# RWKV attention with a routed expert layer on one core: r times the decay prefix on VectorE, half of the diagonals on ScalarE, r times k on GpSimd tied to a VectorE instruction, and the routing spread over two iterations

## The chip, the cores and the metric

The kernel runs on one NeuronCore of a Trainium2 chip. Five engines work side by side, each through a queue of its own in program order: TensorE (PE in the profile, its weight loads PEld), VectorE (DVE), ScalarE (ACT), GpSimd (POOL) and SyncE (SP), which here only issues DMAs. GpSimd issues the indirect DMAs. An instruction waits at the head of its engine's queue until the semaphores it names have been raised, and all behind it waits too. The metric is the device time of one execution in microseconds; the kernel before takes 459.83 us (median of three runs, 458.9 to 461.02).

## What is computed

A linear attention with a decaying state (batch 4, 8 heads, 768 steps, head dimension 48), and on its output a layer of 8 experts of which each token uses one:

```python
for t in range(S):
    cur = np.einsum('bhd,bhe->bhde', u[None] * kt, vt)
    y[:, :, t] = np.einsum('bhd,bhde->bhe', rt, state + cur)
    state = wt[:, :, :, None] * state + np.einsum('bhd,bhe->bhde', kt, vt)
...
logits = x @ w_gate
expert_idx = np.argmax(logits, axis=1)
...
for e in range(E):
    mask = expert_idx == e
...
    xe = x[mask]
    h = np.maximum(xe @ w1[e], 0.0)
    ye = h @ w2[e]
    out[mask] = gate_w[mask, None] * ye
```

## The kernel before

**Stages.** The first 191 us are the attention and the routing, the rest the experts: their weights are split into a high and a low part, tokens are gathered by expert, and the matrix products run back to back on TensorE. The change lies in the first part.

**Blocks.** The 768 steps are cut into 6 chunks of 128, and a chunk of one batch is a block: block n is chunk n // 4 of batch n % 4, 24 in all. A block holds all 8 heads: r, k and w lie as 112 partitions (two heads of a pair at partitions 0 and 64) by 4 pairs by 128 steps. VectorE makes a suffix product of the decays by a scan (`suf`, L331), its reciprocal (L335), `kh` = k times the suffix (L341) and a prefix product from that reciprocal (`pre`, L347). `rh` = r times the prefix (L315) is made by GpSimd but for block 0. TensorE multiplies kh with rh into two PSUM tiles `ap` (L454), one for each head of the pairs. The diagonal of the causal part is another number, r times k times u: GpSimd makes `rk` = r times k (L309), TensorE sums it over the dimension (`cp`, L431), ScalarE copies it (`cs`), TensorE turns it (`cpt`, L437), ScalarE copies it (`ct`), and GpSimd spreads it on the diagonal of `at` by two `affine_select` (L323), one for each half of the heads, with zeros elsewhere. VectorE then copies `ap` into `at` above the diagonal only, by two masked copies (L355). TensorE adds v times `at` (`av`, L488) to `yp`, in which the state's share (`pe_inter`, L466, with `g` from ScalarE) stands already. The state goes on through `kt`, `dp` (L479) and `sst` (L362): `sst` reads `dp` out of PSUM, and kp and dp share two PSUM buffers. ScalarE copies yp to `ytb`, TensorE turns it (`yq`, L495), ScalarE copies that into `xr`, the token rows.

**Order.** `iteration(n)` writes the order out by hand for TensorE, VectorE, ScalarE and GpSimd (`manual_schedule`), n from -3 to 23. One iteration works on several blocks: ap, the masked copies, the state and av of block n, the diagonals of block n + 1, suf, kh and pre of block n + 2, rk of block n + 3. What comes after the loop is placed by the scheduler, which also sets single instructions of it between those of the last iterations.

**Routing.** When a chunk's four blocks are done, its tokens are routed in the next chunk's iterations: at n % 4 == 0 the logits (L502) and `routing` on VectorE (maximum, exponentials on ScalarE, one-hot `oh`, the running counts `oa`, `ohacc`), at n % 4 == 1 `rank` on TensorE (L543 to L546), ahead of pe_inter, and `place` on VectorE, then one indirect scatter of GpSimd (L614) for each batch. From iteration 8 to 20 each iteration also splits a third of a piece of the first expert's weights, the high part by ScalarE, the low part by VectorE (L213).

**Dummy matmuls.** `keep_warm` (L111) issues matmuls of zeros into the unused part of a PSUM tile ahead of cp and of dp: six each in the first blocks, one each later.

## Time and profile before

| What | Value |
|---|---|
| Median of three runs | 459.83 us |
| The profiled execution | 459.9 us |
| Its span, first to last instruction | 458.1 us |
| Busy: PE, DVE, ACT, POOL | 419.8, 296.1, 199.8, 195.9 us |
| Mean granted TensorE clock | 0.934 |
| DMA queues, mean | 137 GB/s |
| First causal matmul of block 0, of block 23 | 15.2 us, 191.4 us |

The chain that ended last, followed back from the end, lies on PE for 68% of the span, on DVE for 13% and on DMA for 10%. In a timeline row stand the start in us, the length in us, the engine, the line, the operation, the tiles (written <- read), the shapes and how often; in brackets how long the engine was idle ahead of it and what ended that. Rows of several equal instructions are merged, and an instruction's length includes its start-up, which overlaps the one before by some 0.1 us; so a step's cost is read from start to start. A GpSimd or VectorE row is also as long as it is if the instruction was held after its start.

### The profile page before, as it was taken

What the parts mean: (1) busy time and instruction counts of PE and PEld (TensorE: products, weight loads), DVE (VectorE), ACT (ScalarE), POOL (GpSimd) and SP (SyncE); (2) the same over time, 40 slices, a digit from 0 to 9 for tenths busy, and PEclk for the clock granted to TensorE, in tenths of its full rate; (3) what the DMA queues carried; (4) which work ended last, traced back from release to release, by engine and by line L of the source; (5) the groups of instructions that cost most, each with busy time, mean ns of one, the idle gap of its engine ahead of it and who ended that gap; (6) DMA issues with size and microseconds to landing.
All of it is one profiled execution on the core that took longest, in us unless ns stands there. A gap on an engine that the chain in (4) does not pass through costs nothing.

```text
span 458.1 us, 9458 instructions
## 1 busy us (share of the span) xinstructions
PE 419.8 (92%) x3608; PEld 368.7 (80%) x3608; DVE 296.1 (65%) x514; ACT 199.8 (44%) x527; POOL 195.9 (43%) x176
## 2 busy tenths in 40 slices
PE   8888899889997996997799999999999999999991
PEld 5566687667765775796699998899999999999991
DVE  5979979999999998444666346345266363632320
ACT  3456455645564473443455344354254352522200
POOL 2998579579579585605401003004002052020530
PEclk9999779889799598799699999999999999999997
DMA  7999757658496314204936334624634455010021
GB/s 209 246 246 232 206 148 195 163 136 204 104 245 146 89 54 153 100 1 140 318 108 200 104 129 130 195 97 115 203 98 149 139 140 156 15 50 0 15 52 37
DMA packets 33178, 62.60 MB, mean 137 GB/s; under 512 B 8086, under 2 KB 21199, under 8 KB 33126
## 3 DMA queue, kind: packets, MB, share of 16 engines
q1 hardware_dynamic: 25222, 52.41, 41.8%
q0 software_dynamic: 7904, 9.52, 6.8%
q8 instruction: 30, 0.49, 0.5%
q14 instruction: 22, 0.18, 0.1%
HBM read 50.03 MB, written 12.29 MB: 136 GB/s over the span
## 4 chain that ended last, share of the span: by engine, by line
PE 68%; DVE 13%; DMA 10%; issue 4%; POOL 2%; SPq 1%; ACT 0%; DVEq 0%; POOLq 0%; ACTq 0%
PE bank L275 25%; PE bank L842 18%; PE opt L287 5%; DMA rkwt<-in_rkw_dram 4%; PE yp L466 4%; PE yp L488 3%; DMA vt<-in_vv_dram 3%; PE ap L454 3%; DVE pre L347 2%; DVE suf L331 2%; PE pt L266 2%; PE yq L495 2%; DVE kh L341 2%; PE op L831 2%; DVE at L355 1%
## 5 line engine op out<-in xcount | busy, mean ns | idle before, releaser
L237 POOL DMA_INDIRECT out_dram<-ot,xg x24 | 36.1, 1504 | 156.3 <-DVE ot L832 150.8
L275 PE MATMUL bank<-xl,w1h 128*128 128x448 f32 (+6 forms) x168 | 59.1, 356 | 0.0
L275 PE MATMUL bank<-xh,w1l 128*128 128x448 f32 (+6 forms) x168 | 58.1, 352 | 0.0
L275 PE MATMUL bank<-xh,w1h 128*128 128x448 f32 (+6 forms) x168 | 56.3, 358 | 0.0
L213 DVE TENSOR_TENSOR w2l<-wst,w2h 128x512 fp32r<-128x512 f32 x48 | 31.3, 685 | 36.5 <-ACT w2h L211 36.3
L278 DVE SCALAR_TENSOR_TENSOR hl<-bank,hh 128x192 fp32r<-128x192 f32 (+8 forms) x58 | 30.7, 539 | 33.1 <-ACT hh L277 33.0
L331 DVE TENSOR_TENSOR_SCAN suf<-rkwt,sufone 112x520 f32<-112x520 f32 x24 | 49.2, 2049 | 3.9 <-DMA rkwt<-in_rkw_dram 3.9
L614 POOL DMA_INDIRECT xs<-xr,pi x24 | 31.5, 1311 | 38.1 <-DVE pi L567 19.7
L277 ACT ACTIVATE hh<-bank 128x192 fp32r<-128x192 f32 (+8 forms) x58 | 26.9, 477 | 41.1 <-PE bank L275 40.8
L315 POOL TENSOR_TENSOR rh<-rkwt,pre 112x512 f32<-112x512 f32 x23 | 36.6, 1591 | 17.8 <-DVE pre L347 17.7
L323 POOL TENSOR_SCALAR_AFFINE_SELECT at<-ct 128x512 f32<-128x512 f32 x48 | 41.2, 881 | 0.0
L842 PE MATMUL bank<-hl,w2h 128*128 128x412 f32 (+5 forms) x114 | 40.8, 359 | 0.0
L842 PE MATMUL bank<-hh,w2l 128*128 128x412 f32 (+5 forms) x114 | 40.6, 358 | 0.0
L842 PE MATMUL bank<-hh,w2h 128*128 128x412 f32 (+5 forms) x114 | 39.8, 355 | 0.0
L309 POOL TENSOR_TENSOR rk<-rkwt 112x512 f32<-112x512 f32 x24 | 35.9, 1498 | 7.7 <-DMA rkwt<-in_rkw_dram 7.7
L355 DVE COPY_PREDICATED at<-cmask,ap 128x512 f32<-128x512 int32 x48 | 32.1, 722 | 7.4 <-PE ap L454 5.1
L488 PE MATMUL yp<-at,vt 128*48 128x128 f32 x384 | 32.6, 308 | 4.7 <-DVE at L355 4.7
L211 ACT ACTIVATE w1h<-wst 128x512 fp32r<-128x512 f32 x48 | 28.5, 627 | 16.4 <-PE bank L275 9.0
L847 ACT ACTIVATE oT<-bank 128x448 f32<-128x448 f32 (+5 forms) x18 | 9.4, 525 | 59.2 <-PE bank L842 59.2
L213 DVE TENSOR_TENSOR w1l<-wst,w1h 128x512 fp32r<-128x512 f32 x48 | 31.1, 686 | 6.4 <-ACT w1h L211 6.3
L347 DVE TENSOR_TENSOR_SCAN pre<-rkwt,pre 112x520 f32<-112x520 f32 x24 | 34.2, 1424 | 0.0
L275 PEld LDWEIGHTS bank<-xl,w1h 128*128 128x128 f32 x168 | 31.6, 188 | 1.1
(157 smaller groups left out, 939.0 us busy)
## 6 DMA issues: line engine op xcount, KB each, us to landing
wst<-in_w_dram SPq DMA_DIRECT2D x48, 256.0 KB, 4.8
...
```

Of the source, the lines that this page charges most:

```text
L213: nc.vector.tensor_tensor(out=lo, in0=st[:, cs], in1=hi.bitcast(F32), op=ALU.subtract)
L237: i = nc.gpsimd.indirect_dma_start(out=out[:, :], out_offset=bass.IndirectOffsetOnAxis(ap=t.bitcast(I32)[:, q, DM + 1:DM + 2], axis=0), in ...
L275: nc.tensor.matmul(hp, a, x[:, j, :], start=(i == 0), stop=(i == 8))
L309: nc.gpsimd.tensor_tensor(out=d["rk"], in0=d["r"], in1=d["k"], op=ALU.mult)
L315: (nc.vector if n == 0 else nc.gpsimd).tensor_tensor(out=d["rh"], in0=d["r"], in1=d["pre"][:, :, 0:C], op=ALU.mult)
L323: nc.gpsimd.affine_select(out=at[:, j], in_=co[:, j:H:2].unsqueeze(2).broadcast_to([P, NP_, C]), pattern=[[0, NP_], [-1, C]], compare_op=A ...
L331: nc.vector.tensor_tensor_scan(out=suf[:, ::-1], data0=d["w"][:, ::-1], data1=sufone.rearrange("p q c -> p (q c)")[:, ::-1], initial=0.0, ...
L347: nc.vector.tensor_tensor_scan(out=pre, data0=d["w"], data1=pre0[n % 2].rearrange("p q c -> p (q c)"), initial=0.0, op0=ALU.mult, op1=ALU.add)
L355: nc.vector.copy_predicated(out=d["at"][:, j], mask=cmask.unsqueeze(1).broadcast_to([P, NP_, C]), data=d["ap"][j])
L488: nc.tensor.matmul(d["yp"][64 * j:64 * j + D, q, :], d["v"][:, h * D:(h + 1) * D], d["at"][:, j, q, :], start=(n < B and q == 0), stop=(q ...
L614: i = nc.gpsimd.indirect_dma_start(out=xsf, out_offset=bass.IndirectOffsetOnAxis(ap=pi[:, b:b + 1], axis=0), in_=xr[:, b, :], in_offset=No ...
L842: nc.tensor.matmul(pp, w, a, start=(i == 0), stop=(i == 23))
```

## The change

- `rh` is made by VectorE for all blocks, at the end of the iteration that makes its prefix (block n + 2), where GpSimd made it an iteration later.
- Of the two diagonals of a block GpSimd makes one. The other is made by ScalarE: four activations, each the identity matrix (128x128) times a number per partition.
- `rk` stands near the head of GpSimd's iteration and, from iteration 0 on, waits for the reciprocal of block n + 2, behind which VectorE's masked copies stand. The diagonal stands behind it.
- `sst` of block n - 1 stands behind the masked copies of block n; it was at the end of iteration n - 1.
- `routing` is cut: the counts and the sums of the exponentials go into a new `count`, in the iteration after, behind the masked copies. `rank` moves behind cp (and its dummies) and ahead of kp. `place` loses what `count` took and moves behind `rh` and the weight split.
- The scatters of a chunk start an iteration later (n % 4 == 2), and two stand in the iteration with n % 4 == 0; the last chunk but one leaves two for after the loop.
- Ahead of cp and dp stand three dummies instead of one in the iterations with n % 4 == 0 and 1.

```diff
@@ pool_rk
-            nc.gpsimd.tensor_tensor(out=d["rk"], in0=d["r"], in1=d["k"], op=ALU.mult)
+            i = nc.gpsimd.tensor_tensor(out=d["rk"], in0=d["r"], in1=d["k"], op=ALU.mult)
+            if real(n - 3):
+                tc.add_manual_dep(i.ins, blk[n - 1]["rc"].name, mybir.DependencyInfo(
+                    mybir.DependencyClass.Sync, mybir.DependencyReason.DATA), reason="beside the copies of the causal part")
@@ pool_rh, now dve_rh
-            (nc.vector if n == 0 else nc.gpsimd).tensor_tensor(out=d["rh"], in0=d["r"], in1=d["pre"][:, :, 0:C], op=ALU.mult)
+            nc.vector.tensor_tensor(out=d["rh"], in0=d["r"], in1=d["pre"][:, :, 0:C], op=ALU.mult)
@@ pool_diag
-            for j in range(2):
-                nc.gpsimd.affine_select(out=at[:, j], in_=co[:, j:H:2].unsqueeze(2).broadcast_to([P, NP_, C]),
-                                        pattern=[[0, NP_], [-1, C]], compare_op=ALU.is_equal, fill=0.0, base=0, channel_multiplier=1)
+            nc.gpsimd.affine_select(out=blk[n]["at"][:, 0], in_=blk[n]["ct"][:, 0:H:2].unsqueeze(2).broadcast_to([P, NP_, C]),
+                                    pattern=[[0, NP_], [-1, C]], compare_op=ALU.is_equal, fill=0.0, base=0, channel_multiplier=1)
+    def act_diag(n):
+        if real(n):
+            for q in range(NP_):
+                nc.scalar.activation(blk[n]["at"][:, 1, q], ident, AF.Copy, scale=blk[n]["ct"][:, 2 * q + 1:2 * q + 2])
@@ pe_coef, pe_state
-            keep_warm(t[:, C:], 6 if n < B else 1)
+            keep_warm(t[:, C:], 6 if n < B else 3 if n % B in (2, 3) else 1)
-            keep_warm(t[:, NP_ * D:], 6 if n < B else 1)
+            keep_warm(t[:, NP_ * D:], 6 if n < B else 3 if n % B < 2 else 1)
@@ iteration
-        pool_rh(n + 1)
         dve_suf(n + 2)
         act_g(n + 1)
-        if route >= 0 and b == 1:
-            rank(route)
+        pool_rk(n + 3)
...
         pe_inter(n)
         dve_at(n)
+        dve_state(n - 1)
+        pool_diag(n + 1)
+        act_diag(n + 1)
...
+        if route >= 0 and b == 1:
+            count(route)
         pe_y(n - 1)
         dve_kh(n + 2)
         act_xr(n - 1)
         pe_coef(n + 2)
...
-        pool_diag(n + 1)
+        if route >= 0 and b == 1:
+            rank(route)
         pe_kt(n + 1)
...
-        pool_rk(n + 3)
-        dve_state(n)
+        dve_rh(n + 2)
```

How this moves the instructions on three engines follows in rows of the built programs: line, operation, tiles, shape of the output, and how often.

VectorE, in the iteration of block 13 (n % 4 == 1), from the masked copies on. Before:

```order
L355 COPY_PREDICATED at<-cmask,ap 128x512 x2
L341 TENSOR_TENSOR kh<-rkwt,suf 112x512
L557 TENSOR_REDUCE se<-ex 128x4
L558 TENSOR_SCALAR se<-se 128x4
L559 RECIPROCAL xr<-se 128x4
L560 COPY xr<-tokid 128x4
L562 TENSOR_TENSOR ps<-rank,ebase 128x32
L563 TENSOR_TENSOR ps<-ps,oh 128x32
L565 TENSOR_REDUCE pf<-ps 128x4
L567 CAST pi<-pf 128x4
L347 SCALAR_TENSOR_TENSOR pre<-rkwt,pre_1_177 112x520
```

After:

```order
L361 COPY_PREDICATED at<-cmask,ap 128x512 x2
L368 TENSOR_TENSOR sst_186<-dp,gbd_185 112x192
L541 CAST oa<-ohacc 128x8
L543 TENSOR_REDUCE ohs<-oh 128x8
L544 TENSOR_TENSOR ohacc<-ohacc,ohs 128x8
L546 TENSOR_REDUCE se<-ex 128x4
L547 TENSOR_SCALAR se<-se 128x4
L548 RECIPROCAL xr<-se 128x4
L549 COPY xr<-tokid 128x4
L347 TENSOR_TENSOR kh<-rkwt,suf 112x512
L353 SCALAR_TENSOR_TENSOR pre<-rkwt,pre_1_177 112x520
L319 TENSOR_TENSOR rh<-rkwt,pre 112x512
```

The state's update and the counts have come behind the copies, rh behind the prefix; the four instructions that read rank have gone from here to behind rh and the weight split.

GpSimd, with what each instruction waits for in brackets (DVE_49, PE_49 and the like are engines, DMAHW queues of loads). Before, from the first scatter of chunk 1 at the end of iteration 9 through iteration 10:

```order
L614 DMA xs<-xr,pi 24576x386 [waits DVE_49]
L315 TENSOR_TENSOR rh<-rkwt,pre 112x512 [waits DVE_49,Pool_49]
L323 AFFINE_SELECT at<-ct 128x512 [waits PE_49,Activation_49]
L323 AFFINE_SELECT at<-ct 128x512
L309 TENSOR_TENSOR rk<-rkwt 112x512 [waits DMAHW7_49,DMAHW0_49]
```

After, iteration 12 with its two scatters, and the head of the next:

```order
L309 TENSOR_TENSOR rk<-rkwt 112x512 [waits DMAHW5_49,DMAHW6_49,DVE_49,Pool_49]
L624 DMA xs<-xr,pi 24576x386
L325 AFFINE_SELECT at<-ct 128x512 [waits PE_49,Activation_49]
L624 DMA xs<-xr,pi 24576x386
L309 TENSOR_TENSOR rk<-rkwt 112x512 [waits DMAHW3_49,DMAHW4_49,DVE_49,Pool_49]
```

rh and one diagonal are gone, and rk, which waited for its block's load alone, has moved from behind the diagonals to the head and waits for VectorE (the reciprocal) as well.

TensorE, at the rank matmuls of the iteration of block 13. Before:

```order
L488 MATMUL yp<-at,vt 48x128 x8
L454 MATMUL ap<-rh,kh 128x128 x8
L543 LDWEIGHTS tri
L543 MATMUL rank<-oh,tri 128x32
L544 LDWEIGHTS ones
L544 MATMUL rank<-oa,ones 128x32
```

After, from the third dummy ahead of cp on (inter, yq and two dummies stand before these rows):

```order
L111 LDWEIGHTS ones
L111 MATMUL cp<-wz,ones 128x384
L437 MATMUL cp<-rk,ubt 32x128 x4
L559 LDWEIGHTS tri
L559 MATMUL rank<-oh,tri 128x32
L560 LDWEIGHTS ones
L560 MATMUL rank<-oa,ones 128x32
```

Rank stood directly behind ap, ahead of the block's other matmuls; now inter, yq, three dummies and cp stand ahead of it.

More of the change, by code (lines that the diff above doesn't have):

```diff
@@ L308, in pool_rk, with dve_rh @@
             d["rk"] = wk.tile([RP, NP_, C], F32, name="rk", tag="rk", bufs=4)
-            nc.gpsimd.tensor_tensor(out=d["rk"], in0=d["r"], in1=d["k"], op=ALU.mult)
-    def pool_rh(n):
+            i = nc.gpsimd.tensor_tensor(out=d["rk"], in0=d["r"], in1=d["k"], op=ALU.mult)
+            if real(n - 3):
+                tc.add_manual_dep(i.ins, blk[n - 1]["rc"].name, mybir.DependencyInfo(
+                    mybir.DependencyClass.Sync, mybir.DependencyReason.DATA), reason="beside the copies of the causal part")
+    def dve_rh(n):
         if real(n):
@@ L314, in pool_rh @@
             d["rh"] = wk.tile([RP, NP_, C], F32, name="rh", tag="rh", bufs=3)
[L315 removed]
+            nc.vector.tensor_tensor(out=d["rh"], in0=d["r"], in1=d["pre"][:, :, 0:C], op=ALU.mult)
     def pool_diag(n):
         if real(n):
[L320 to L325 removed]
+            blk[n]["at"] = wk.tile([P, 2, NP_, C], F32, name="at", tag="at")
+            nc.gpsimd.affine_select(out=blk[n]["at"][:, 0], in_=blk[n]["ct"][:, 0:H:2].unsqueeze(2).broadcast_to([P, NP_, C]),
[4 more added lines that the diff above has]
+                nc.scalar.activation(blk[n]["at"][:, 1, q], ident, AF.Copy, scale=blk[n]["ct"][:, 2 * q + 1:2 * q + 2])
     def dve_suf(n):
@@ L334, in dve_suf @@
             d["suf"] = suf.rearrange("p (q c) -> p q c", c=WP)
-            nc.vector.reciprocal(pre0[n % 2][:, :, 0:1], d["suf"][:, :, 1:2])
+            d["rc"] = nc.vector.reciprocal(pre0[n % 2][:, :, 0:1], d["suf"][:, :, 1:2]).ins
     def dve_kh(n):
@@ L528, in routing, with count @@
                                        op0=ALU.min, op1=ALU.is_equal)
+        ch["r", c] = (ex, oh)
+    def count(c):
+        ex, oh = ch["r", c]
+        xr = ch["xr", c]
         oa = sm.tile([P, E], BF16, name="oa", tag="oa")
@@ L533, in routing @@
         nc.vector.tensor_tensor(out=ohacc, in0=ohacc, in1=ohs, op=ALU.add)
-        ch["r", c] = (ex, oh, oa)
+        se = sm.tile([P, B], F32, name="se", tag="se")
+        nc.vector.tensor_reduce(out=se, in_=ex, axis=AX.X, op=ALU.add)
+        nc.vector.tensor_scalar(out=se, in0=se, scalar1=1e-9, scalar2=None, op0=ALU.add)
+        nc.vector.reciprocal(xr[:, :, DM], se)
+        nc.vector.tensor_copy(xr.bitcast(I32)[:, :, DM + 1], tokid[:, c, :])
+        ch["r", c] = (oh, oa)
     def rank(c):
-        ex, oh, oa = ch["r", c]
+        oh, oa = ch["r", c]
         rk = psX.tile([P, B + 1, E], F32, name="rank", tag="tp")
@@ L549, in place @@
     def place(c):
-        xr = ch["xr", c]
-        ex, oh, oa = ch["r", c]
+        oh, oa = ch["r", c]
         rk = ch["rank", c]
@@ L555, in place @@
         rk = rk[:, 0:B, :]
-        se = sm.tile([P, B], F32, name="se", tag="se")
-        nc.vector.tensor_reduce(out=se, in_=ex, axis=AX.X, op=ALU.add)
-        nc.vector.tensor_scalar(out=se, in0=se, scalar1=1e-9, scalar2=None, op0=ALU.add)
-        nc.vector.reciprocal(xr[:, :, DM], se)
-        nc.vector.tensor_copy(xr.bitcast(I32)[:, :, DM + 1], tokid[:, c, :])
         ps = sm.tile([P, B, E], F32, name="ps", tag="ps")
@@ L663, in iteration @@
         pe_a(n)
-        pool_rh(n + 1)
         dve_suf(n + 2)
         act_g(n + 1)
-        if route >= 0 and b == 1:
-            rank(route)
+        pool_rk(n + 3)
+        if n in (6, 7):
+            scatter(0, (2 * n - 12,))
+        if route > 1 and b == 0:
+            scatter(route - 1, (2,))
+        if route > 0 and b > 1:
+            scatter(route, (b - 2,))
         pe_inter(n)
         dve_at(n)
+        dve_state(n - 1)
+        pool_diag(n + 1)
+        act_diag(n + 1)
+        if n in (6, 7):
+            scatter(0, (2 * n - 11,))
+        if route > 1 and b == 0:
+            scatter(route - 1, (3,))
+        if route >= 0 and b == 1:
+            count(route)
         pe_y(n - 1)
@@ L677, in iteration @@
             logit_mm(route)
-        if n in (6, 7):
-            scatter(0, (2 * n - 12,))
-        pool_diag(n + 1)
+        if route >= 0 and b == 1:
+            rank(route)
         pe_kt(n + 1)
         act_kt(n + 1)
-        if route >= 0 and b == 1:
-            place(route)
         dve_pre(n + 2)
@@ L698, in iteration @@
             routing(route)
+        if route >= 0 and b == 1:
+            place(route)
         act_junk(n + 2)
@@ L704, in iteration @@
         pe_av(n)
-        if route > 0 and b > 0:
-            scatter(route, (b - 1,))
-        if route > 1 and b == 0:
-            scatter(route - 1, (3,))
-        if n in (6, 7):
-            scatter(0, (2 * n - 11,))
         if n == 0:
@@ L729, in rwkv_moe_kernel @@
         act_y(NB - 1)
-    scatter(NCH - 2, (3,))
+    scatter(NCH - 2, (2, 3))
     nl = NB - 1
@@ L745, in rwkv_moe_kernel @@
     routing(NCH - 1)
+    count(NCH - 1)
     rank(NCH - 1)
```

3 lines of the change are left out of this document (removed).

## The prediction

> **What bounds the kernel now.** I read the windows view first, cut where the causal matmuls (L454) of blocks 0, 4, 8, 12, 16, 20 and 23 start, so that each row but the last two is one round of four iterations. Columns: stretch, its length, busy time of each engine (instructions), granted TensorE clock, DMA share, GB/s.
>
> ```profile
> core 0: us, PE busy (x) PEld busy (x) DVE busy (x) ACT busy (x) POOL busy (x), PEclk, DMA share, GB/s
> 15.20:42.30 27.10, 24.21 (x299) 17.54 (x299) 24.44 (x31) 14.57 (x45) 26.65 (x35) 1.00 1.00 237
> 42.30:73.50 31.20, 29.03 (x375) 22.78 (x374) 28.58 (x46) 16.28 (x55) 21.05 (x19) 0.84 0.75 195
> 73.50:105.40 31.90, 28.27 (x378) 22.00 (x376) 31.42 (x47) 17.38 (x59) 24.09 (x20) 0.89 0.59 151
> 105.40:136.90 31.50, 28.48 (x378) 21.90 (x376) 30.74 (x48) 18.16 (x61) 22.88 (x21) 0.89 0.74 191
> 136.90:168.80 31.90, 28.64 (x371) 22.50 (x370) 31.09 (x50) 16.55 (x57) 25.36 (x21) 0.84 0.39 100
> 168.80:191.40 22.60, 18.27 (x223) 14.45 (x219) 17.43 (x42) 9.63 (x36) 15.51 (x16) 0.77 0.36 118
> 191.40:458.00 266.60, 251.24 (x1511) 239.68 (x1509) 122.30 (x239) 101.78 (x209) 53.53 (x36) 0.97 0.37 113
> ```
>
> After 191.4 us TensorE is busy 251 of 267 us, and the change touches nothing there. The three rounds from 73.5 to 168.8 keep VectorE busy 31.42, 30.74 and 31.09 of some 31.8 us: VectorE is the bound. What it does in that time shows the timeline of VectorE in the iteration of block 12, and GpSimd's beside it:
>
> ```profile
> 105.84 0.68 DVE L213 TENSOR_TENSOR w1l<-wst,w1h 128x512 fp32r<-128x512 f32 x1
> 106.44 2.24 DVE L331 TENSOR_TENSOR_SCAN suf<-rkwt,sufone 112x520 f32<-112x520 f32 x1
> ...
> 109.17 1.36 DVE L355 COPY_PREDICATED at<-cmask,ap 128x512 f32<-128x512 int32 x2 [0.27 <-POOL at L323]
> 110.42 1.07 DVE L341 TENSOR_TENSOR kh<-rkwt,suf 112x512 f32<-112x512 f32 x1
> ...
> 112.82 0.68 DVE L213 TENSOR_TENSOR w1l<-wst,w1h 128x512 fp32r<-128x512 f32 x1
> ```
> ```profile
> 105.83 1.73 POOL L315 TENSOR_TENSOR rh<-rkwt,pre 112x512 f32<-112x512 f32 x1 [0.41 <-DVE pre L347]
> 107.51 2.18 POOL L323 TENSOR_SCALAR_AFFINE_SELECT at<-ct 128x512 f32<-128x512 f32 x2
> 109.67 1.27 POOL L309 TENSOR_TENSOR rk<-rkwt 112x512 f32<-112x512 f32 x1
> ```
>
> The same VectorE instructions one iteration on, where GpSimd is idle up to 121.7 us:
>
> ```profile
> 116.90 1.23 DVE L331 TENSOR_TENSOR_SCAN suf<-rkwt,sufone 112x520 f32<-112x520 f32 x1
> ...
> 118.25 1.32 DVE L355 COPY_PREDICATED at<-cmask,ap 128x512 f32<-128x512 int32 x2
> 119.48 0.67 DVE L341 TENSOR_TENSOR kh<-rkwt,suf 112x512 f32<-112x512 f32 x1
> 120.07 0.17 DVE L557 TENSOR_REDUCE se<-ex 128x4 f32<-128x32 f32 x1
> ...
> 121.37 1.24 DVE L347 TENSOR_TENSOR_SCAN pre<-rkwt,pre 112x520 f32<-112x520 f32 x1
> 122.52 0.33 DVE L362 TENSOR_TENSOR sst<-dp,gbd 112x192 f32<-112x192 f32 x1
> 122.77 0.68 DVE L213 TENSOR_TENSOR w1l<-wst,w1h 128x512 fp32r<-128x512 f32 x1
> 123.36 4.80 DVE L331 TENSOR_TENSOR_SCAN suf<-rkwt,sufone 112x520 f32<-112x520 f32 x1
> ```
> ```profile
> 123.46 1.19 POOL L315 TENSOR_TENSOR rh<-rkwt,pre 112x512 f32<-112x512 f32 x1
> 124.59 1.22 POOL L323 TENSOR_SCALAR_AFFINE_SELECT at<-ct 128x512 f32<-128x512 f32 x2
> 125.79 1.26 POOL L309 TENSOR_TENSOR rk<-rkwt 112x512 f32<-112x512 f32 x1
> ```
>
> The suffix scan takes 1.23 us alone and 2.24 beside rh; it ends 1.1 after rh does. At 123.36 it takes 4.80 and ends 1.1 after the last of four GpSimd instructions in a row. kh goes from 0.67 to 1.07 beside rk. The masked copies out of PSUM (1.36 beside rk and a diagonal, 1.32 alone) do not care. So a VectorE instruction with two inputs in SBUF and a GpSimd instruction exclude each other, and copies out of PSUM stand outside. From start to start an iteration without GpSimd costs VectorE: scan and reciprocal 1.35, two copies 1.23, kh 0.59, pre 1.15, sst 0.25, weight split 0.59, together **5.16 us**. In block 12 the same list took 112.82 − 105.84 = 6.98: 1.8 us of it is GpSimd.
>
> **The change, part by part.**
>
> *rh on VectorE.* It has the shape of kh and its price, 0.59 us from start to start: 5.75 with the weight split (blocks 8 to 19), 5.16 without. GpSimd loses an instruction of 1.19 us.
>
> *One diagonal to ScalarE.* Four 128x128 activations with a scale per partition are in no row of before. The nearest row is four of 112x48:
>
> ```profile
> 106.40 1.00 ACT L384 ACTIVATE gbd<-sst,wtot 112x48 f32<-112x48 f32 x4
> ```
>
> 1.0 is the lower end, 2.0 (twice as long for 2.7 times the columns) the upper; I take 1.3. ScalarE is busy 17.38 of 31.9 us a round; 4 x 1.3 makes it 22.6, under what VectorE and TensorE need below. They stand ahead of xr and cs; TensorE wants cs only after kp, the dummy matmul and dp, so I charge nothing. At 2.0 cs could come 0.7 us later in each iteration, 2.8 a round; TensorE's 26.4 (below) would be 29.2, 1.0 over VectorE.
>
> *rk beside the copies.* rk waits for the reciprocal and then takes 1.27 us, the copies 1.23 and sst 0.25: nothing for VectorE. The wait holds up GpSimd's queue, the diagonal and the scatters behind it; but GpSimd, busy 22.88 in the round from 105.4, loses 4 x (1.19 + 0.61) = 7.2 us, so it is idle before most reciprocals and the diagonal is not wanted before the next iteration.
>
> *The diagonal that stays* follows rk, or a scatter behind rk, and then lies beside kh, pre or rh: 0.61 us an iteration if GpSimd goes first, nothing if VectorE does, 1.88 if a VectorE instruction that came first is held through rk and diagonal, as the scan at 123.36 was. I take 0.6, since in the rows a waiting GpSimd instruction came in at the next boundary (107.51, behind the scan).
>
> The page "SBUF — State Buffer" of the Trainium skill, section "Who interferes with whom", says that the second to issue blocks until the first finishes. By that a collision costs one GpSimd instruction at most, 0.61 us here, and the sum below stands; the 4.80 us scan, held through four, disagrees, and the measurement decides.
>
> *Routing split over two iterations.* In before all of it stands in one iteration, with the rank matmuls at the head of TensorE's next block:
>
> ```profile
> 113.85 0.75 DVE L523 SCALAR_TENSOR_TENSOR cd<-sh,iom 128x32 f32<-128x32 f32 x1
> ...
> 115.09 0.65 DVE L530 CAST oa<-ohacc 128x8 bf16<-128x8 f32 x1
> ...
> 115.88 1.09 DVE L533 TENSOR_TENSOR ohacc<-ohacc,ohs 128x8 f32<-128x8 f32 x1
> ```
> ```profile
> 115.23 0.19 PE L543 MATMUL rank<-oh,tri 128*128 128x32 bf16 x1 [1.78 <-DVE oh L527]
> ```
> ```profile
> 178.42 0.19 DVE L523 SCALAR_TENSOR_TENSOR cd<-sh,iom 128x32 f32<-128x32 f32 x1
> ...
> 179.12 0.16 DVE L530 CAST oa<-ohacc 128x8 bf16<-128x8 f32 x1
> ...
> 179.47 0.17 DVE L533 TENSOR_TENSOR ohacc<-ohacc,ohs 128x8 f32<-128x8 f32 x1
> ```
>
> VectorE spends 116.90 − 112.82 − 0.59 = 3.49 us on the first part and 121.37 − 120.07 = 1.30 on the second. The three instructions above exceed their times alone by 0.56 + 0.49 + 0.92 = 1.97, because they lie beside GpSimd: a round's routing falls from 4.8 to 2.8 us. TensorE's 1.78 us wait for the one-hot goes: rank now stands behind inter, yq and cp, and its last input is written one cast behind the copies. What is late next is dp: its buffer is now released by sst one iteration later, behind the same copies. From the copies' start sst ends at 1.5. In block 12 cp starts at 108.27 and the next ap at 112.30 (rows below); without the logits' 1.2 that is 2.8 us for cp, kp, dummy, dp, cpt and av, so what follows sst, with an ap behind it, is an estimated 4 us at most: 1.5 + 4 = 5.5, before VectorE is back at its copies 5.75 later.
>
> *Dummy matmuls.* Four more in each of two iterations per round. From the rows of block 12:
>
> ```profile
> 67.80:73.50 5.70, 5.70 (x86) 4.50 (x84) 5.67 (x6) 3.77 (x15) 5.50 (x5) 1.00 0.97 221
> ...
> 105.40:112.30 6.90, 6.87 (x121) 5.49 (x119) 6.59 (x9) 3.92 (x15) 6.33 (x6) 1.00 0.93 233
> ```
> ```profile
> 108.01 0.33 PE L111 MATMUL cp<-wz,ones 128*128 128x384 bf16 x1
> 108.27 0.43 PE L431 MATMUL cp<-rk,ubt 112*32 112x128 f32 x8
> ```
>
> A plain iteration needs 5.7 us of TensorE, one with logits 6.9, rank some 0.3, a dummy 0.26. A round: 4 x 5.7 + 1.2 + 0.3 + 8 x 0.26 = **26.4 us**.
>
> *The end of the loop.* The copy of token numbers waited there for a scatter's landing:
>
> ```profile
> 177.90 0.17 DVE L560 COPY xr<-tokid 128x4 int32<-128x4 int32 x1 [0.98 <-DMA xs<-xr,pi]
> ```
>
> It still stands in block 20's routing, and the scatter that it waits for is GpSimd's last instruction of that iteration; I give it about 0.5 us more. The rest of that stretch is one chain through VectorE. Of 22.6 us I take 1.6 off: less contention, less of a routing wait.
>
> **Sum.** Rounds with the split: VectorE 4 x (5.75 + 0.6) + 2.8 = 28.2, over TensorE's 26.4; with 0.3 for handing over (VectorE idled 0.5 to 0.8 us in these rounds before) 28.5. Savings: 3.4, 3.0, 3.4. Round from 42.3: VectorE 4 x 5.76 + 2.8 = 25.8, TensorE 26.4, with 0.6 for handing over 27.0: 4.2. First round: GpSimd is the bound, 26.65 of 27.1, and falls to 19.4; TensorE's 24.21, its dummies included, is next: 24.5, saving 2.6. The end 1.6. Together 18.2 us. The profiled execution took 459.9 us, 1.8 more than its span and level with the median of 459.83: 459.9 − 18.2 = **441.7 us**.
>
> **Rivals.**
>
> *TensorE becomes the bound:* GpSimd gives way, the 0.6 goes, VectorE needs 25.8 a round and TensorE with its dummies 26.4 + 0.6. For it: the masked copies' window nearly holds rk and diagonal. Against it: they need 1.88 us, the window has 1.5. Three rounds at 27.0 instead of 28.5: 437.2.
>
> *DMA holds the first rounds:* the DMA engines are busy 1.00 of the first round at 237 GB/s, so a faster loop could wait for blocks there. Then the 2.6 goes, and 2 of the next 4.2: 446. Against it: the loads run ahead by up to six blocks.
>
> *Half the contention stays:* where rk starts late, rk and diagonal fall on kh and a scan. Half of the chain's extra 1.28 us in 20 blocks is 12.8, less 1.2 that TensorE's bound hides in the second round: 453.3.
>
> *Slower:* every iteration loses the whole chain, 1.88 us instead of 0.6, at kh. It decides once GpSimd is not free when the reciprocal comes, that is when its own iteration is longer than VectorE's. Rounds of 33.6 (three), 30.9, and an end 3.8 later: 15.3 + 3.9 + 3.8 = 23.0 more than forecast, 465. Against it: GpSimd's 22.88 us, less 7.2, in a round of 28.
>
> *The wait does not order rk* (rk goes where it went): then kh pays as before, 0.4 in each of 20 blocks, 450; counted with the half.
>
> **How the numbers follow.** Forecast 0.56 (438 to 445), TensorE bound 0.16, DMA 0.09, half the contention or something between it and the slower case 0.13, slower 0.06. The range 434.5 to 453.5 takes in all but the last; its low end is TensorE's bound with no handing over (0.6 in four rounds and 0.3 in the first less). About 0.5% is what a measurement of this kernel can tell from no change; no case ends within it, and 0.03 is left for one between the half and the slower: faster 0.91, same 0.03, slower 0.06.
>
> **What would show it.** Right: suf near 1.25 us in its mean (2.05 now), kh and rh near 0.7, rk starting right behind each reciprocal, no wait of rank over 0.5 us, rounds near 28. The single diagonal should be found in gaps between kh, pre and rh. Wrong: scans of over 2 us, ScalarE late with cs or ytb, waits of TensorE for ytb or of VectorE for ap (TensorE is then the bound), or blocks waiting for rkwt.

## The result and the profile after

The changed kernel takes **445.76 us** (median of 4 executions, 444.14 to 449.33), the kernel before 460.42 beside it: a ratio of 0.969, with a 95% interval of 0.9615 to 0.9764. Forecast were 441.7 us and a range of 434.5 to 453.5. A few executions of the runs below fell in a slower state (one of `both`, 444.13 us, one of `routing_back`, 449.4, and some of the kernel before); the ratios leave them out, the medians keep them.

The profiled execution took 446.88 us, its span 445.2. The windows view of the changed kernel, cut as in the prediction (length, busy time of each engine, granted TensorE clock, DMA share, GB/s):

```profile
14.61:40.59 25.98, 23.91 (x300) 17.27 (x299) 25.63 (x38) 18.98 (x61) 13.13 (x27) 1.00 1.04 230
40.59:68.97 28.38, 25.62 (x384) 19.96 (x382) 23.75 (x47) 20.76 (x73) 10.27 (x10) 1.00 0.94 235
68.97:96.54 27.57, 25.93 (x385) 19.98 (x383) 26.91 (x52) 21.14 (x75) 12.58 (x13) 1.00 0.69 169
96.54:124.22 27.68, 25.99 (x384) 19.97 (x382) 27.06 (x53) 21.46 (x76) 13.85 (x12) 1.00 0.82 213
124.22:151.15 26.93, 25.41 (x381) 19.61 (x379) 26.35 (x52) 20.93 (x75) 13.13 (x11) 1.00 0.47 120
151.15:176.51 25.36, 18.97 (x223) 15.22 (x221) 17.04 (x45) 12.86 (x48) 9.54 (x11) 0.80 0.33 107
176.51:445.20 268.69, 251.67 (x1511) 239.92 (x1509) 122.34 (x239) 101.79 (x209) 54.31 (x37) 0.97 0.37 113
```

| stretch, from block | before | forecast | after | after less forecast |
|---|---|---|---|---|
| 0 | 27.1 | 24.5 | 26.0 | +1.5 |
| 4 | 31.2 | 27.0 | 28.4 | +1.4 |
| 8, 12, 16 | 31.9, 31.5, 31.9 | 28.5 each | 27.6, 27.7, 26.9 | −3.3 together |
| 20 to 22 | 22.6 | 21.0 | 25.4 | +4.4 |
| 23 to the end | 266.6 | 266.6 | 268.7 | +2.1 |

With block 0 starting 0.6 us sooner this makes 5.5 us more than forecast (445.2 against the forecast's span of 439.9). The rounds in which VectorE is the bound came out better than forecast, the others worse; the stretch from block 20 to 22 and what follows it are even longer than before (25.4 against 22.6 us, 268.7 against 266.6). The granted clock of the rounds, 0.84 to 0.89 before in four of them, is 1.00.

The groups of VectorE's, GpSimd's and ScalarE's instructions (busy time, mean ns of one, idle time ahead of them) answer to what the prediction wanted to see:

```profile
L337 DVE TENSOR_TENSOR_SCAN suf<-rkwt,sufone 112x520 f32<-112x520 f32 x24 | 30.1, 1253 | 3.3 <-DMA rkwt<-in_rkw_dram 3.3
L319 DVE TENSOR_TENSOR rh<-rkwt,pre 112x512 f32<-112x512 f32 x24 | 20.9, 872 | 0.8
L347 DVE TENSOR_TENSOR kh<-rkwt,suf 112x512 f32<-112x512 f32 x24 | 20.4, 849 | 0.0
L309 POOL TENSOR_TENSOR rk<-rkwt 112x512 f32<-112x512 f32 x24 | 32.7, 1362 | 76.9 <-issue 49.0
L331 ACT ACTIVATE at<-ident,ct 128x128 f32<-128x128 f32 x96 | 30.4, 390 | 0.1
```

The suffix scan's mean is 1.25 us, as hoped; kh and rh came to 0.85 and 0.87 us, not 0.7. A regular iteration, that of block 14, on VectorE and then on GpSimd:

```profile
112.88 1.24 DVE L337 TENSOR_TENSOR_SCAN suf<-rkwt,sufone 112x520 f32<-112x520 f32 x1
114.16 0.18 DVE L341 RECIPROCAL pre<-suf 112x4 f32<-112x4 f32 x1
114.25 1.34 DVE L361 COPY_PREDICATED at<-cmask,ap 128x512 f32<-128x512 int32 x2
115.50 0.33 DVE L368 TENSOR_TENSOR sst<-dp,gbd 112x192 f32<-112x192 f32 x1
115.76 0.67 DVE L347 TENSOR_TENSOR kh<-rkwt,suf 112x512 f32<-112x512 f32 x1
116.35 1.23 DVE L353 TENSOR_TENSOR_SCAN pre<-rkwt,pre 112x520 f32<-112x520 f32 x1
```
```profile
114.48 1.29 POOL L309 TENSOR_TENSOR rk<-rkwt 112x512 f32<-112x512 f32 x1 [6.23 <-issue]
115.92 1.41 POOL L624 DMA_INDIRECT xs<-xr,pi  x1 [0.15 <-DVE sst L368]
117.34 0.67 POOL L325 TENSOR_SCALAR_AFFINE_SELECT at<-ct 128x512 f32<-128x512 f32 x1
```

rk starts 0.14 us behind the reciprocal's end, beside the copies, which take what they took. The scatter lies beside kh and pre and costs neither anything. The diagonal costs VectorE 0.26 us, the 0.95 of the rh that it meets (one stands at 157.71 below) over the 0.69 of others.

Where the time was lost shows VectorE in the iteration of block 20, then GpSimd ahead of it and TensorE behind it:

```profile
157.71 0.95 DVE L319 TENSOR_TENSOR rh<-rkwt,pre 112x512 f32<-112x512 f32 x1
...
159.39 0.19 DVE L525 TENSOR_TENSOR sh<-lpt,mx 128x32 f32<-128x32 f32 x1
165.26 0.17 DVE L549 COPY xr<-tokid 128x4 int32<-128x4 int32 x1 [5.68 <-DMA xs<-xr,pi]
```
```profile
157.43 0.67 POOL L325 TENSOR_SCALAR_AFFINE_SELECT at<-ct 128x512 f32<-128x512 f32 x1
158.27 1.88 POOL L624 DMA_INDIRECT xs<-xr,pi  x1 [0.17 <-issue]
```
```profile
168.67 0.17 PE L557 MATMUL rank<-oa,ones 128*128 128x8 bf16 x1 [3.51 <-DVE oa L541]
```

The copy of chunk 5's token numbers goes into the buffer from which chunk 3's last scatter, issued at 158.27, still reads; it landed 6.9 us later. That is no accident of this execution: in five of the profiles below the scatter at this place took 6.7 to 7.1 us to land. Before, it took 3.0, and the copy waited 0.98. And GpSimd, then VectorE, in iterations 6 and 7:

```profile
63.32 1.17 POOL L624 DMA_INDIRECT xs<-xr,pi  x1 [5.22 <-DMA rkwt<-in_rkw_dram]
64.52 0.65 POOL L325 TENSOR_SCALAR_AFFINE_SELECT at<-ct 128x512 f32<-128x512 f32 x1
```
```profile
61.84 0.18 DVE L341 RECIPROCAL pre<-suf 112x4 f32<-112x4 f32 x1
65.20 1.34 DVE L361 COPY_PREDICATED at<-cmask,ap 128x512 f32<-128x512 int32 x2 [3.18 <-POOL at L325]
```

Chunk 0's first scatter waits 5.22 us for DMAs (the view names a load of `rkwt`; which one it was is open); the diagonal behind it in GpSimd's queue is late, and with it the masked copies.

### The profile page after: what moved, and what is told of

Its sections match the earlier page's. It is cut to its first block, busy times and chain, and to the rows that moved or that the text cites. A ratio compares the mean times of both kernels' runs of the same rounds, so it can differ in the third digit from the quotient of the medians.

```text
span 445.2 us, 9604 instructions
## 1 busy us (share of the span) xinstructions
PE 408.8 (92%) x3643; PEld 359.4 (81%) x3644; DVE 279.2 (63%) x537; ACT 224.6 (50%) x623; POOL 132.4 (30%) x129
## 4 chain that ended last, share of the span: by engine, by line
PE 62%; DVE 16%; DMA 11%; issue 5%; SPq 2%; POOL 1%; ACT 1%; POOLq 0%; DVEq 0%; ACTq 0%
PE bank L275 26%; PE bank L858 19%; DMA rkwt<-in_rkw_dram 6%; PE opt L287 5%; DVE suf L337 4%; DMA vt<-in_vv_dram 3%; DVE pre L353 3%; DVE at L361 2%; DMA xs<-xr,pi 2%; PE pt L266 2%; PE yp L494 2%; DVE kh L347 2%; PE op L847 2%; PE yp L472 1%; PE ap L460 1%
## 5 line engine op out<-in xcount | busy, mean ns | idle before, releaser
L309 POOL TENSOR_TENSOR rk<-rkwt 112x512 f32<-112x512 f32 x24 | 32.7, 1362 | 76.9 <-issue 49.0
L277 ACT ACTIVATE hh<-bank 128x192 fp32r<-128x192 f32 (+8 forms) x58 | 26.9, 477 | 41.1 <-PE bank L275 40.9
L211 ACT ACTIVATE w1h<-wst 128x512 fp32r<-128x512 f32 x48 | 28.5, 627 | 16.6 <-PE bank L275 9.1
L275 PEld LDWEIGHTS bank<-xl,w1h 128*128 128x128 f32 x168 | 31.6, 188 | 1.1
L275 PEld LDWEIGHTS bank<-xh,w1l 128*128 128x128 f32 x168 | 31.6, 188 | 1.1
L275 PEld LDWEIGHTS bank<-xh,w1h 128*128 128x128 f32 x168 | 31.2, 188 | 1.3 <-ACT xh L267 0.2
L337 DVE TENSOR_TENSOR_SCAN suf<-rkwt,sufone 112x520 f32<-112x520 f32 x24 | 30.1, 1253 | 3.3 <-DMA rkwt<-in_rkw_dram 3.3
L331 ACT ACTIVATE at<-ident,ct 128x128 f32<-128x128 f32 x96 | 30.4, 390 | 0.1
L353 DVE TENSOR_TENSOR_SCAN pre<-rkwt,pre 112x520 f32<-112x520 f32 x24 | 30.0, 1250 | 0.0
```

Source lines behind the costliest of these rows:

```text
L211: nc.scalar.activation(hi, st[:, cs], AF.Copy)
L275: nc.tensor.matmul(hp, a, x[:, j, :], start=(i == 0), stop=(i == 8))
L309: i = nc.gpsimd.tensor_tensor(out=d["rk"], in0=d["r"], in1=d["k"], op=ALU.mult)
L331: nc.scalar.activation(blk[n]["at"][:, 1, q], ident, AF.Copy, scale=blk[n]["ct"][:, 2 * q + 1:2 * q + 2])
L337: nc.vector.tensor_tensor_scan(out=suf[:, ::-1], data0=d["w"][:, ::-1], data1=sufone.rearrange("p q c -> p (q c)")[:, ::-1], initial=0.0, ...
L353: nc.vector.tensor_tensor_scan(out=pre, data0=d["w"], data1=pre0[n % 2].rearrange("p q c -> p (q c)"), initial=0.0, op0=ALU.mult, op1=ALU.add)
```

## The experiments

Each kernel ran six to twelve times beside the kernel before on the same chip; the runs are of three chips (up to `rk_free`, up to `routing_back`, the rest), on which the kernel before took 460.95, 461.28 and 461.17 us. The ratio is to that kernel, and runs on different chips are compared by it. Each profile is of one execution only; where that one lies far from the median, the text says so.

| kernel | median us | ratio, 95% interval |
|---|---|---|
| token_copy | 440.27 | 0.9546 (0.9505 to 0.9588) |
| diag_first | 445.78 | 0.9674 (0.9628 to 0.972) |
| both | 440.19 | 0.9564 (0.9518 to 0.961) |
| rk_free | 452.88 | 0.982 (0.9775 to 0.9864) |
| one_dummy | 443.28 | 0.9588 (0.9532 to 0.9645) |
| rh_pool | 438.45 | 0.9501 (0.9461 to 0.9541) |
| diag_pool | 448.1 | 0.972 (0.9671 to 0.9768) |
| routing_back | 443.56 | 0.9603 (0.9555 to 0.9652) |
| rh_late | 461.82 | 0.9992 (0.9957 to 1.0026) |
| spread | 438.05 | 0.949 (0.9459 to 0.9521) |
| spread_one | 438.72 | 0.9497 (0.9467 to 0.9526) |
| spread_rh | **434.77** | 0.9418 (0.9382 to 0.9455) |

### The two waits

**token_copy**

```diff
-    xrp = actx.enter_context(tc.tile_pool(name="xrp", bufs=2))
+    xrp = actx.enter_context(tc.tile_pool(name="xrp", bufs=3))
```

> Edit on the changed kernel: a third buffer for xr, so that the copy of chunk 5's token numbers no longer waits for the landing of chunk 3's last scatter. Theory: that wait (5.68 us in the profile of the changed kernel, at 159.6, VectorE idle, then TensorE cold and 3.51 us of rank's wait behind it) is the mis-sized term of the end of the loop. With it gone the stretch from block 20 to block 23 falls from 25.4 us to 20 to 21.5, the total by 4 to 5 us: about 441 against 445.8. Rival 1: something else is late next there (the scatter itself, ytb on ScalarE, the rows of the first expert), the stretch falls by less than 2 us: 444 to 446. Rival 2: the wait is an accident of that one execution (the scatter took 6.9 us to land there, 3.0 in the kernel before); then the stretch falls in the profile but the median by only 1 to 2 us: 444.

440.27 us. The windows view of its stretch from block 20 to block 23:

```profile
149.73:168.64 18.91, 15.26 (x223) 11.87 (x221) 17.51 (x44) 12.78 (x48) 7.33 (x8) 1.00 0.43 132
```

18.9 us instead of 25.4, at a granted clock of 1.00 instead of 0.80: with the wait goes rank's wait of 3.51 us behind it. The theory holds, and the stretch fell more than expected; the medians moved by 5.5 us, their intervals do not meet.

**diag_first**

```diff
-        if n in (6, 7):
-            scatter(0, (2 * n - 12,))
...
         pool_diag(n + 1)
         act_diag(n + 1)
         if n in (6, 7):
-            scatter(0, (2 * n - 11,))
+            scatter(0, (2 * n - 12, 2 * n - 11))
```

> Edit on the changed kernel: in iterations 6 and 7 the diagonal of the next block goes ahead of chunk 0's scatter on GpSimd. Theory: the first scatter waits 5.22 us for the zero rows' DMAs and the diagonal behind it holds VectorE's copies for 3.2 us and, through the buffer of dp, TensorE for 2.56; with the diagonal ahead both waits go, iteration 7 falls from 8.47 us to about 6 and the round from 40.6 from 28.4 to about 26; total about 2.4 us less: 443.3 against 445.8. Rival: rk of block 10, which then stands behind the waiting scatter, or the DMA engines, which are 0.94 busy in this round, take the place of the wait: the round stays over 27.5 us, the total within 1 us of 445.8.

445.78 us: nothing gained, the rival's number, though iterations 6 and 7 take 5.75 us each in its profile (5.76 and 8.47 in the changed kernel). Iteration 9 takes 8.64 instead of 7.50, and in iteration 7 a prefix scan took 3.11 us: two scatters behind one another make GpSimd late, and its rk and diagonal come upon the scan. In that profile (443.75 us) this takes back 1.1 of the 4.0 us by which the first two rounds are shorter; why the median kept nothing of the rest is open. The expectation's reason for the wait, the zero rows, is doubtful: the last of them was issued at 45.60, the one before it had landed by 52.25, and the scatter began at 63.32.

**both**

> Both edits in one kernel (third buffer for xr, diagonal ahead of chunk 0's scatter). The waits lie in different rounds, so the theory has their gains add: 438.5 to 439.5 us, 21 less than the kernel before, rounds 26, 28.4 -> 26, and 20 to 21.5 at the end. Rival: they share a cause behind them (DMA or TensorE), and the two together give no more than the better of them, 441 or more.

440.19 us, between the theory's 439.5 and the rival's 441, and like token_copy: the diagonal ahead adds nothing to the median. It is the base of the next five runs, with the token copy's wait out of the way. Its profile is of its fastest execution, 436.45 us.

### Parts of the change undone

**rk_free** (both edits, and `if real(n - 3)` ahead of rk's dependency made `if False`)

> The kernel with both edits, but rk no longer waits for the reciprocal: the order on every engine is the same, GpSimd starts rk as soon as its queue comes to it. Theory: a VectorE instruction with two inputs in SBUF and a GpSimd instruction exclude each other, and the copies out of PSUM stand outside. Then rk's 1.27 us falls on rh, the weight split or the suffix scan instead of the copies: the mean of suf rises from 1.25 us to 1.5 or more, each iteration is 0.6 to 1.2 us longer, the rounds from 69 us go from 27.5 to 30 or more, and the total is 9 to 20 us over the kernel with both edits, some 12 as one value: 451. Rival: the placement is worth nothing, since TensorE (26.0 us busy in these rounds of 27.6) is almost the bound and one GpSimd instruction more in the gaps finds room: 0 to 2 us over the kernel with both edits.

452.88 us, 12.7 over its base; the theory's "some 12". Its group row of the suffix scan:

```profile
L337 DVE TENSOR_TENSOR_SCAN suf<-rkwt,sufone 112x520 f32<-112x520 f32 x24 | 37.7, 1570 | 3.9 <-DMA rkwt<-in_rkw_dram 3.9
```

With the same order on every engine, where rk falls is worth 12.7 us. Not all of it is exclusion. To count that, sum over VectorE's instructions from 14 us to block 23 the time by which each exceeds what a tenth of its kind stay under (over all 14 profiles, excesses of 0.05 us and more): 16.6 us here, 9.6 with both edits. That is 7.0 of the 17.1 us between the two profiles' spans. TensorE loses time too: its granted clock is 0.88, 0.93 and 0.96 in the first, the fourth and the fifth round and 0.84 behind them, where it is 1.00 with both edits. The first round alone is 4.8 us longer (29.3 us). VectorE is late there with sst, for which the matmuls of zeros ahead of dp wait, and the matmuls behind that wait take nearly twice as long; the second row is the same place in the changed kernel:

```profile
27.18 1.78 PE L111 MATMUL dp<-wz,ones 128*128 128x320 bf16 x6 [1.79 <-DVE sst L370]
```
```profile
25.87 0.99 PE L111 MATMUL dp<-wz,ones 128*128 128x320 bf16 x6 [1.20 <-DVE sst L370]
```

**diag_pool** (both edits, `pool_diag` writes both diagonals, `act_diag` is not called)

> The kernel with both edits, with both diagonals on GpSimd and none on ScalarE. Theory: rk fills the window of the copies out of PSUM, so the second diagonal (0.61 us) falls on kh or the prefix scan: 0.6 us an iteration if one boundary more is lost, 1.2 if a VectorE instruction is held through both: total 452 (440.2 + 20 x 0.6), bounds 448 to 464; mean of kh or pre 0.5 us or more longer. Rival: GpSimd has the room (13 us busy of 27.6) and the ScalarE work that goes (1.3 us an iteration) makes up for it: total within 3 us of 440.2.

448.1 us, 7.9 over its base, at the lower bound. It is no even charge. In its profile (450.74 us, against the base's 436.45) the three rounds from block 8 are 3.0 us longer, 0.25 us an iteration instead of 0.6; the first round is 5.0 longer and the stretch from block 20 to 22 3.9, at granted clocks of 0.88 and 0.78. The mean of the suffix scan rises to 1.39 us, of the prefix scan to 1.34, not by the 0.5 expected.

**rh_pool**

```diff
-            nc.vector.tensor_tensor(out=d["rh"], in0=d["r"], in1=d["pre"][:, :, 0:C], op=ALU.mult)
+            (nc.vector if n == 0 else nc.gpsimd).tensor_tensor(out=d["rh"], in0=d["r"], in1=d["pre"][:, :, 0:C], op=ALU.mult)
...
+        dve_rh(n + 1)
         dve_suf(n + 2)
...
-        dve_rh(n + 2)
```

> The kernel with both edits, with rh back on GpSimd at the head of the iteration, where it lies beside the weight split and the suffix scan. Theory: exclusion makes the place, not the engine, decide: VectorE saves rh (0.87 us from start to start with the collision on it) and the suffix scan beside rh takes 2.24 instead of 1.23 us as in the kernel before, so that an iteration gains or loses little, 0.1 to 0.5 us more: total 442 to 450, as one value 444. Rival 1: moving rh is the main part of the change's gain: 0.9 us an iteration and more, 455 or more. Rival 2: work taken off the bound engine is a gain whatever it lies beside: 436 or less.

438.45 us: no slower than with rh on VectorE. The expected 444 was too high by 5.5 us, and the first rival is out, and so is the second (436 or less). VectorE and GpSimd in its iteration of block 15:

```profile
116.97 1.67 DVE L337 TENSOR_TENSOR_SCAN suf<-rkwt,sufone 112x520 f32<-112x520 f32 x1
118.67 0.18 DVE L341 RECIPROCAL pre<-suf 112x4 f32<-112x4 f32 x1
118.77 1.35 DVE L361 COPY_PREDICATED at<-cmask,ap 128x512 f32<-128x512 int32 x2
120.01 0.33 DVE L368 TENSOR_TENSOR sst<-dp,gbd 112x192 f32<-112x192 f32 x1
120.27 1.14 DVE L347 TENSOR_TENSOR kh<-rkwt,suf 112x512 f32<-112x512 f32 x1
```
```profile
116.23 1.31 POOL L325 TENSOR_SCALAR_AFFINE_SELECT at<-ct 128x512 f32<-128x512 f32 x1
117.52 2.10 POOL L319 TENSOR_TENSOR rh<-rkwt,pre 112x512 f32<-112x512 f32 x1
119.58 1.27 POOL L309 TENSOR_TENSOR rk<-rkwt 112x512 f32<-112x512 f32 x1
```

The scan waits for the diagonal's end (1.67 instead of 1.24), then goes ahead of rh; rh is the one held, 2.10 instead of 1.19, and its work falls beside the copies. That costs VectorE 0.43, and kh 0.47 (1.14 instead of 0.67) beside the late rk; rh on VectorE costs it 0.61 to 0.87. Over the whole loop it comes out even: counted as above VectorE's excess is 23.5 us here and 9.6 with both edits, and the 13.9 between are just what 23 rh at 0.61 cost it (14.0).

**routing_back** (both edits; `oa`, `ohs`, `ohacc` behind `routing`, rank ahead of inter, place and the gate's reciprocal ahead of the prefix scan)

> The kernel with both edits, with the routing's instructions in the places of the kernel before (count behind routing in the same iteration, rank at the head of TensorE's next block, place and the gate's reciprocal ahead of the prefix scan). Theory: its cost before the change was 1.97 us a round of exclusion with GpSimd, which does not come back, since GpSimd is idle there now, and rank's wait of 1.78 us on TensorE, which does, of which the slack of TensorE (1.6 us a round) hides most: rounds 0.2 to 1 us longer, total 441 to 445, as one value 443. Rival 1: the spread is worth the 2 us a round of the forecast and more: 449 or more. Rival 2: it is worth nothing now: 439.5 to 441.

443.56 us, 3.4 over its base (443.29 without its longest execution of 449.4), with intervals that overlap. In its profile the four stretches from block 8 take 29.0, 27.3, 27.0 and 19.5 us against 28.0, 27.7, 26.9 and 18.9: 1.3 together; the other 4.0 us between the two spans lie elsewhere. The theory's 443 fits; a gain of the spread is likely but is not settled.

**one_dummy** (both edits, one matmul of zeros instead of three)

> The kernel with both edits, with one dummy matmul instead of three in each place from block 4 on, as before the change: TensorE has 8 x 0.26 = 2.1 us less in a round. Theory: VectorE is the bound of the rounds from 69 us, TensorE's clock is kept by its real work since rank no longer makes it wait: rounds stay within 0.5 us, granted clock over 0.95 there, total 439 to 441 (440.2 with both edits). Rival 1: the dummies hold the clock (it was 0.84 to 0.89 in these rounds before the change, 1.00 after) and that is where part of the gain came from: the clock falls under 0.9 again, rounds 1 us and more longer, total 444 or more. Rival 2: TensorE is the bound (7.41 us busy of 7.41 in the iterations with logits): rounds 1 us and more shorter, total under 437.

443.28 us, 3.1 over its base, with intervals that overlap. The granted clock fell to 0.89 and 0.94 in two rounds, as the first rival has it, but VectorE has long instructions there too:

```profile
65.25 3.13 DVE L337 TENSOR_TENSOR_SCAN suf<-rkwt,sufone 112x520 f32<-112x520 f32 x1
...
70.01 2.35 DVE L347 TENSOR_TENSOR kh<-rkwt,suf 112x512 f32<-112x512 f32 x1
72.28 1.67 DVE L353 TENSOR_TENSOR_SCAN pre<-rkwt,pre 112x520 f32<-112x520 f32 x1
```

From them a chain of waits leads to TensorE: ScalarE's exponentials wait 3.3 us for VectorE's `sh`, ytb stands behind them, TensorE waits 3.57 us for it at 77.0, and its granted clock is 0.72 over that iteration. But the stretch from block 20, in which VectorE has no such hold, has a clock of 0.76 too and takes 21.7 us instead of 18.9.

### What makes an instruction wait so long

These long ones (4.80 before the change, 3.13, 2.35) have a thing in common: they begin shortly before GpSimd ends the issue of a scatter and goes on at once with another instruction. Beside the 4.80 us scan of the prediction, which begins at 123.36 in the kernel before, stands on GpSimd:

```profile
121.74 1.69 POOL L614 DMA_INDIRECT xs<-xr,pi  x1 [4.79 <-DVE pi L567]
123.46 1.19 POOL L315 TENSOR_TENSOR rh<-rkwt,pre 112x512 f32<-112x512 f32 x1
```

I counted this in the profiles of all 14 kernels, for scans, kh, rh and the weight split, where the next GpSimd instruction follows the scatter within 0.06 us and VectorE's instruction is then still running:

| VectorE's instruction begins before the scatter's end by | cases | over its time alone |
|---|---|---|
| up to 0.64 us | 14 | 0.47 to 3.57 us, every one |
| 0.66 us | 2 | 0 and 1.75 us |
| 0.76 to 1.06 us | 113 | 0.02 us at most |

In the kernel before four such holds cost VectorE 2.47, 3.56, 3.57 and 1.16 us, 10.8 together; the changed kernel's profile has none, since its scatters end 0.96 to 0.99 us into the prefix scan. The tests:

**rh_late** (on the kernel before; `iteration` calls `dve_suf` ahead of `pool_rh`, since rh now waits for that scan's reciprocal)

```diff
+            if n - 1 in (10, 14, 18):
+                tc.add_manual_dep(i.ins, blk[n + 1]["rc"].name, mybir.DependencyInfo(
+                    mybir.DependencyClass.Sync, mybir.DependencyReason.DATA), reason="behind the scan")
```

> Edit on the kernel before, nothing else of the change in it: in iterations 10, 14 and 18 GpSimd's rh waits for the reciprocal behind the suffix scan. There a scatter of xs ends 0.06 to 0.07 us into the scan and rh, two diagonals and rk follow it at once; the scan took 4.79, 4.80 and 2.39 us instead of 1.23. Theory: a VectorE instruction that begins at the end of a scatter's issue is passed by all GpSimd instructions that follow at once, and this, not the regular collision, is most of what GpSimd cost the kernel before. Then the scans take 1.23 us, rh lies beside the copies, the diagonal and rk fall on kh and the prefix scan one boundary at a time (0.5 to 1 us an iteration), and the total falls by 4 to 8 us of 460.5, as one value 455. Rival 1: the exclusion takes the same time wherever the four GpSimd instructions stand: within 2 us of the kernel before. Rival 2: the later chain makes kh and the masked copies of the next block late and the kernel slower.

461.82 us: no gain, the first rival's number. The three scans do take 1.23 us, and two rounds fall, from 31.8 to 29.4 and from 32.0 to 28.2. But the round between them grows from 31.5 to 36.3, and the last stretch from 22.5 to 26.4. VectorE and GpSimd in iteration 13, and VectorE in iteration 21:

```profile
111.10 4.21 DVE L526 SCALAR_TENSOR_TENSOR cd<-sh,iom 128x32 f32<-128x32 f32 x1
```
```profile
110.35 1.30 POOL L617 DMA_INDIRECT xs<-xr,pi  x1 [0.16 <-issue]
111.67 1.19 POOL L315 TENSOR_TENSOR rh<-rkwt,pre 112x512 f32<-112x512 f32 x1
```
```profile
179.28 0.17 DVE L563 COPY xr<-tokid 128x4 int32<-128x4 int32 x1 [5.27 <-DMA xs<-xr,pi]
```

The hold moved: a routing instruction of 0.19 us, begun 0.55 us before a scatter's end, waited through rh, both diagonals and rk. And the token copy, come to earlier, waited 5.27 us. Counted as above VectorE's excess is 40.1 us, against 41.7 in the kernel before: what the three scans no longer lost, other instructions lost. That is the first rival's mechanism, so the theory's gain of 4 to 8 us is not shown. The rows show that the holds come and go with the phase of the two engines.

**spread** (the kernel with both edits)

```diff
-        if n in (6, 7):
-            scatter(0, (2 * n - 12, 2 * n - 11))
+        if n in (7, 8, 9):
+            scatter(0, ((0,), (1, 2), (3,))[n - 7])
```

> Edit on the kernel with both edits: chunk 0's scatters stand behind the diagonal of iterations 7 (one), 8 (two) and 9 (one) instead of two each in 6 and 7. Theory: two scatters in one iteration (1.3 to 1.8 us each) make GpSimd late for the next reciprocal; rk then begins right at a scatter's end and kh and the prefix scan of iterations 7 to 9 are held (1.41, 1.67 and 1.60 us in the profile of the kernel with both edits; a scan of 3.11 us with the diagonal ahead alone). With GpSimd in time these go: iterations 7 to 9 together 20.6 us instead of 21.1, and the executions spread less; total 438 to 439.5 against 440.2. Rival: the scatters lose the same time wherever they stand, 440 to 441.

438.05 us, 2.1 under its base, with intervals that just overlap. The executions spread from 437.25 to 439.73 (436.45 to 440.98 in the base, and the one of 444.13). Iterations 7 to 9 take 5.75, 7.41 and 6.81 us, 20.0 together, better than expected.

**spread_one** (the same edit on one_dummy)

> The kernel with both edits and one dummy matmul (443.3), with chunk 0's scatters spread as in the run beside it. Theory: the 3 us that one dummy cost came from VectorE instructions held behind scatters in iterations 7 to 9 (a scan of 3.13, kh of 2.35 us), a matter of phase and not of the clock, and go with them: 439 to 441. Rival: they come from the clock, which the dummies hold (0.89 granted in that round, 1.00 with three dummies): still 443 or more.

438.72 us, level with spread: most of what one dummy had cost went without the dummies, and the median does not reach the rival's 443. The rival's cause is not out, though. The granted clock is lower in every execution (0.960 to 0.970 over the whole of it, 0.972 to 0.978 with three dummies). The profile is of the one execution of 443.01 us; its stretch from block 20 takes 21.7 us at a clock of 0.76, 19.4 at 0.91 in the profile with three. So the dummies hold the clock up here, and what that is worth in the median, 0.7 us here, is inside the noise.

**spread_rh** (the same edit on rh_pool)

> The kernel with both edits and rh back on GpSimd (438.5), with chunk 0's scatters spread as in the run beside it. Theory: as in that run, kh of iterations 7 and 8 (1.84 and 2.37 us in the profile with rh back) is no longer held: 436 to 438, the fastest of all. Rival: with rh on GpSimd there are four instructions of it in an iteration, so one more scatter in an iteration is what is late, and it is no better than 438.5 to 440.

**434.77 us**, the fastest: faster than spread, with intervals that just do not meet, and faster than the kernels before and after the change. Four of its six executions took 433.98 to 435.16 us; the profile is of the longest, 440.26, in which the first round takes 31.6 us (25.8 in rh_pool), at a granted clock of 0.84, behind a wait of 2.37 us of TensorE for sst. The windows view of its rounds from blocks 8, 12 and 16:

```profile
73.10:100.05 26.95, 25.91 (x384) 20.04 (x382) 26.01 (x47) 21.02 (x75) 20.40 (x18) 1.00 0.74 182
100.05:126.84 26.79, 25.84 (x385) 19.97 (x383) 26.31 (x49) 21.37 (x76) 21.69 (x17) 1.00 0.89 229
126.84:153.30 26.46, 25.41 (x380) 19.62 (x378) 25.99 (x49) 20.85 (x75) 21.27 (x17) 1.00 0.44 120
```

VectorE and TensorE are both within 1.1 us of the round's length.

## Why the prediction was right, and where it was not

*Bound and mechanism: right.* VectorE's excess, counted as under rk_free, fell from 41.7 us to 9.1. The prediction's 1.8 us for each of 23 iterations were 41. Less 23 rh at 0.61, which VectorE took over, 18.6 of these 32.6 us remain; block 23 comes 14.9 us sooner (191.4 to 176.5). TensorE's clock rose with it, from 0.84 to 0.89 to 1.00 in four rounds: its wait for rank once a round, behind which it had been lower, is gone. The sum had no term for the clock, and how much of the gain runs through it is open. But the 1.8 us were no even charge: 10.8 of the 41.7 lay in four holds behind scatters. By the Trainium skill's page "SBUF — State Buffer", section "Who interferes with whom", as the prediction read it, a collision costs one GpSimd instruction at most; scans passed by four of them in two iterations of the kernel before disagree.

*rh on VectorE: the price was right, the gain was not there.* The sum had rh's 0.59 as the price of an iteration without its collision; with rk and one diagonal out of the way rh on GpSimd costs no more, and in the best version 3.3 us less (434.77 against 438.05).

*rk beside the copies: right*, the largest part, 12.7 us when undone, though VectorE's excess is only 7.0 of the 17.1 us in the profiles. *One diagonal to ScalarE: right*, 7.9 us when undone; four activations take 4 x 0.29 from start to start, 1.2 where 1.3 was forecast, and ScalarE is busy 21.5 of 27.7 us. It is late once a round, 1.0 us for TensorE's inter (78.52, 106.21, 133.90), in iterations that VectorE fills (7.2 to 7.3 of 7.5 us); 0.7 of it is its own wait for VectorE's `sh`. How the 7.9 us divide between exclusion and TensorE's clock is open.

*The diagonal that stays: over-sized.* 0.6 us an iteration were forecast, 0.26 to 0.47 came, mostly behind a scatter where it met rh. With this the three rounds were forecast 3.3 us too long.

*Routing: right in direction.* Rank, which waited for the one-hot once a round, waits no more within the rounds. What the spread is worth alone, 1.3 us by the profile and 3.4 by the medians, is not settled. *Dummy matmuls:* counted right as work; they hold the clock up, and in the median that is not measurable (438.72 against 438.05).

*The end of the loop: the mis-sized term.* "About 0.5 us more" for the token copy's wait were 4.7 more (5.68 against 0.98), and 1.6 off became 2.8 on. The prediction saw the wait and priced it by the scatter's issue; VectorE had come earlier, the scatter took 6.9 us to land instead of 3.0, and TensorE's rank waited 3.51 us behind it. token_copy shows it: 18.9 us without the wait, under the forecast's 21.0.

*The first two rounds: 2.9 us too short.* In the second the wait of chunk 0's scatter was not seen, because before the change it did not wait there. Putting the diagonal ahead gives a second round of 25.7 us in the profile of the kernel with both edits, but no time in the median; a first round of 24.5 came there too. In the first round of the changed kernel VectorE is busy 25.63 of 25.98 us, its rh and scans at 1.58 to 1.67 beside GpSimd: the forecast had TensorE as the bound there and no collisions. In part they come from loads: rk waited 1.36 and 1.60 us for its blocks' rows (14.77, 18.83), so it or the diagonal behind it fell on rh, the scans and kh. The rival of DMA in the first rounds was right in that much.

The rival of a TensorE bound was half right: in the three rounds the iterations with logits have TensorE busy 7.42 of 7.42, 7.49 of 7.51 and 7.49 of 7.51 us, the others not (5.98 of 6.45, for one).
